# Attention in pairs of head pairs on quadrants of the PE array, and a last product with 512 tokens moving

## The chip, the cores and the metric

The kernel runs on one core of a Trainium2 chip. Times are device microseconds (us) of one execution. The runs shown are three, with median 1648.64 us (1648.32 to 1651.41); a profile of one further execution gives the instructions of each engine: PE (matmul), PEld (weight load), DVE (vector), ACT (scalar), POOL, and SP, whose queue issues the DMAs. PE, DVE, ACT and SP each work through a list of their own in order; semaphores tie the lists together.

## What is computed

The shapes are: 8 batches, 8 heads, 576 tokens, head size 64; then 4608 tokens of width 512, a first MLP of width 2048 and a gated second one of width 1536.

```python
def _attn_ref(q, k, v):
    q_s = softmax(q, axis=-1); k_s = softmax(k, axis=2)
    kv = np.einsum('bhsd,bhse->bhde', k_s, v)
    return np.einsum('bhsd,bhde->bhse', q_s, kv)
x = attn_out.transpose(0, 2, 1, 3).reshape(4608, 512)
x = np.maximum(x @ moe_w_in, 0.0) ** 2 @ moe_w_out
out = (1 / (1 + np.exp(-(x @ moe2_w_gate))) * (x @ moe2_w_val)) @ moe2_w_out
```

The `softmax` here stands for the maximum, the exponential, the sum with 1e-9 and the division that the reference writes out. The weights arrive as 64-bit floats.

## The kernel before, in words

**The order of the work.** Every piece of work is given to a planner (`Plan`) with a due time, its cost on an engine, what it must follow and which buffers it takes and gives. `plan.trace()` plays a clock through this list and emits the instructions in the order that comes out, so each engine's list, SP's included, is fixed when the program is built. The `plan_*` functions hold these due times and costs. `SIZES` says how many buffers each tag has; `W` is the pool of 512 KB weight buffers, eleven of them, and `X` and `S` are the pools of split activations.

**Numbers.** A float32 matrix is split into a high and a low part (ACT writes the high one, DVE the low one). A product is then three matmuls (`mm3`, L218 to L220) into one PSUM bank. Big products run as seven block products in place of eight (`PRODUCTS`, `plan_seven`); `s1`, `s5`, `s2` and `p4` are the four blocks of a result, of which `p4` ends last.

**Attention** (L408 to L676) goes in blocks: `j` counts nine blocks of 512 tokens, `b` eight batches, `p` four pairs of heads. For one (b, p), `plan_k` takes the column maximum of k (`k_max`, a PE transpose `k_turn`, `k_col`, a PE broadcast `k_all`), subtracts, exponentiates, and `k_mm` (L472) multiplies k by v: for each head the stationary matrix has 128 rows and 64 columns, so the two heads of the pair stand on the two column halves of the array. `k_copy` writes the two 64x64 results, scaled, on the diagonal of a 128x128 tile `kvf` whose other half is zero. For one (j, p), `plan_q` does the softmax of q on DVE and ACT; for j of 2 and more a head is spread over two groups of partitions, and `q_swap` (L534) brings the other group's maximum or sum by a small matmul. `q_mm` (L595) multiplies `kvf` by q: one full-array float32 matmul per piece of batch.

**The MLPs.** Blocks 0 to 2 go through the first MLP by `conv_in` and `conv_out`, while the weights are still being converted. The other six go in three stages (`in_stage`), with the attention of later blocks set between their matmuls. Five stages of the second MLP follow (`gate_stage`); four have 1024 tokens and the last 512. The end of a gate stage is `p_out2` (L736): y is stationary (128 tokens), a row block of `w_out2` moves, 256 columns at a time. Its results lie with tokens on partitions; `z_copy` and `z_st` (L942, L945) store them.

Of the kernel before, what the change touches and what calls it, by code (L numbers as in the profile page):

```python
# [142 lines left out]
def attention_mlp_mlp(  # L143
# [20 lines left out]
    nc = tc.nc  # L164
# [13 lines left out]
    SIZES = {"X": 14, "W": 11, "S": 6, "f": 19, "x": 8, "q": 3, "a": 6, "w": 5, "k": 2, "v": 2, "km": 1, "kr": 2, "pa": 2, "cb": 2, "qm": 4, "qr": 4}  # L178
# [12 lines left out]
    kvf = [[cst.tile([128, 128], F32, name=f"kv{a}{p}") for p in range(NP)] for a in range(2)]  # L191
# [233 lines left out]

# [6 lines left out]

    def k_max(b, p, r):

        kt = kt_t[b, p].rearrange("p r c -> p (r c)")
        C = 2 * D
        if r == 0:
            mx = cst.tile([128, 2 * C], F32, tag="kmx", name="kmx")
            nc.vector.tensor_tensor(out=mx, in0=kt[:, 0:2 * C], in1=kt[:, 2 * C:4 * C], op=ALU.max)
            kmx[b, p] = mx  # L440
            return
        a, c = kmx[b, p][:, 0:C], kmx[b, p][:, C:2 * C]
        nc.vector.tensor_tensor(out=a, in0=a, in1=kt[:, 4 * C:5 * C] if r == 1 else c, op=ALU.max)
        if r == 2:
            kmx[b, p] = a

    def k_turn(b, p):
        ps = banks[p] if b == 0 else pa.tile([128, N], F32, tag="pa", name="kps")
        nc.tensor.transpose(ps[:, KT0:KT0 + 128], kmx[b, p], ident)  # L449
        kps[b, p] = ps  # L450

    def k_col(b, p):

        m1 = sp.tile([128, 1], F32, tag="km1", name="km1")
        nc.vector.tensor_reduce(out=m1, in_=kps[b, p][:, KT0:KT0 + 128], axis=AX.X, op=ALU.max)
        kmx[b, p] = m1

# [14 lines left out]
    def k_mm(b, p):  # L472
        kt, vt = kt_t.pop((b, p)), vt_t.pop((b, p))
        ps = kps[b, p]
        for r in range(RK):
            for h in range(2):
                c = VC * r + (D + 2 if h else 1)
                nc.tensor.matmul(  # L478
                    ps[D * h:D * h + D, D - D * h:2 * D + 1 - D * h], kt[:, r, D * h:D * h + D], vt[:, c:c + D + 1],
                    start=(r == 0), stop=(r == RK - 1), skip_group_check=True,  # L480
                )

    def k_rec(b, p):
        ri = sp.tile([128, 1], F32, tag="kri", name="kri")
        nc.vector.tensor_scalar(out=ri, in0=kps[b, p][:, D:D + 1], scalar1=1e-9, scalar2=None, op0=ALU.add)
# [3 lines left out]
    def k_copy(b, p):  # L489
        ps, ri = kps.pop((b, p)), kmx.pop((b, p))  # L490
        for h in range(2):
            s = slice(D * h, D * h + D)
            c = slice(0, D) if h else slice(D + 1, 2 * D + 1)
            nc.scalar.activation(out=kvf[b % 2][p][s, s], in_=ps[s, c], func=AF.Copy, scale=ri[s])
# [47 lines left out]
    def q_both(j, p, op):  # L542
        st = q_st[j, p]
        n = N // qu_cols(j)
        s2 = st.rearrange("p g o -> p (g o)")
        if j >= NPE:
            nc.vector.tensor_tensor(out=s2, in0=s2, in1=q_ps.pop((j, p))[:, 0:n], op=op)
        return st, s2

    def q_sub(j, p):  # L550
        n = qu_cols(j)
        t = q_t[j, p].rearrange("p (g d) -> p g d", d=n)
        mx, _ = q_both(j, p, ALU.max)
        nc.vector.tensor_tensor(out=t, in0=t, in1=mx.to_broadcast([128, N // n, n]), op=ALU.subtract)
# [18 lines left out]
    def q_mul(j, p):  # L573
        n = qu_cols(j)
        t = q_t[j, p].rearrange("p (g d) -> p g d", d=n)
        nc.vector.tensor_tensor(out=t, in0=t, in1=q_rec.pop((j, p)).to_broadcast([128, N // n, n]), op=ALU.mult)

    def q_turn(j, p):
        t = tile2("a", "qtr")
        nc.vector.transpose(out=t, in_=q_t.pop((j, p)))  # L580
        q_ps[j, p] = t

    def q_turn_pe(j, p):
        t = q_t.pop((j, p)).rearrange("p (r c) -> p r c", r=R)
# [35 lines left out]
    SLACK = 2.14  # L620
    slack = lambda j: SLACK if j > 4 else 0.0

    def plan_k(b, p, key, step, wait=()):
        n = (b, p)
        big = ("W", "W") if b == 0 else ("k", "v")
        bank = [] if b == 0 else ["pa"]
        add(key - 5 if b else p, {DMA: 0.92}, ("kt",) + n, k_load, b, p, after=wait, take=big[:1])
        add(key - 4 if b else p + 4, {DMA: 0.92}, ("vt",) + n, v_load, b, p, after=wait, take=big[1:])
        add(key + 2.5 * step, {ACT: 0.22}, ("vo",) + n, v_ones, b, p, after=[("vt",) + n])
        add(key, {DVE: 0.34}, ("km0",) + n, k_max, b, p, 0, after=[("kt",) + n], take=["km"])  # L630
        add(key + 0.1, {DVE: 0.21}, ("km1",) + n, k_max, b, p, 1, after=[("km0",) + n])
        add(key + 0.2, {DVE: 0.21}, ("kmx",) + n, k_max, b, p, 2, after=[("km1",) + n])
        add(key + 0.5 * step, {PE: 0.14}, ("kt2",) + n, k_turn, b, p, after=[("kmx",) + n], take=bank, slack=slack(b))
        add(key + step, {DVE: 0.22}, ("kdg",) + n, k_col, b, p, after=[("kt2",) + n])
        add(key + 1.5 * step, {PE: 0.25}, ("kgm",) + n, k_all, b, p, after=[("kdg",) + n], give=["km"], slack=slack(b))
        add(key + 2 * step, {DVE: 0.74}, ("ks",) + n, k_sub, b, p, after=[("kgm",) + n])
        add(key + 3 * step, {ACT: 0.64}, ("ke",) + n, k_exp, b, p, after=[("ks",) + n])
        add(key + 4 * step, {PE: 0.65}, ("kp",) + n, k_mm, b, p, after=[("ke",) + n, ("vo",) + n], give=big, slack=slack(b))
        add(key + 5 * step, {DVE: 0.35}, ("kr",) + n, k_rec, b, p, after=[("kp",) + n], take=["kr"])
        add(  # L640
            key + 6 * step, {ACT: 0.65}, ("kv",) + n, k_copy, b, p,
# [763 lines left out]
```

## Time and profile before

| what | value |
|---|---|
| median of 3 runs | 1648.64 us |
| the profiled execution, its own time | 1648.78 us |
| its span, first instruction to last | 1647.0 us |
| PE busy | 1619.0 us, 98% |
| DVE busy | 1225.3 us, 74% |
| ACT busy | 942.4 us, 57% |
| DMA | 462.14 MB, mean 281 GB/s |
| HBM read and written | 364.54 MB, 95.94 MB |

The 1.8 us between the profiled time and its span lie before the first and behind the last instruction. A matmul's end in the profile is modelled and overlaps the next one, so the rate of PE is read from one start to the next and not from the durations. A float32 matmul stands in the profile as two matmuls (two passes), an `mm3` as three.

### The profile page before, as it was taken

To read this page: it belongs to the slowest core of one execution; us is meant where nothing else is said; L and a number is where in the kernel's file an instruction comes from. 1 tells how busy PE (TensorE), PEld (TensorE's weight loads), DVE (VectorE), ACT (ScalarE), POOL (GpSimd) and SP (SyncE) were. 2 spreads that over 40 slices of the span, in tenths; PEclk is the share of its full clock that TensorE was granted. 3 is DMA by queue.
4 is the path that set the end of the run, shared out by engine and by line. 5 is a ranking of instruction groups with operands and counts; after the bars stand their busy time and mean duration, and the time that the engine had idled before them with its cause. 6 is when DMAs were issued, how large, how long until landed. Compare 5 with 4: busy or idle time off the path is not lost.

```text
span 1647.0 us, 24974 instructions
## 1 busy us (share of the span) xinstructions
PE 1619.0 (98%) x8964; PEld 1377.5 (84%) x8964; DVE 1225.3 (74%) x2279; ACT 942.4 (57%) x1706; POOL 1.9 (0%) x14
## 2 busy tenths in 40 slices
PE   6899999999999999999999999999999999999999
PEld 4678888888888887888788899888988899889998
DVE  7988675999999999987996785447724783458446
ACT  5887665569585867675864464335523553335344
POOL 0000000000000000000000000000000000000000
PEclk8999999999999999999999999999999999999999
DMA  7695999999899979899989877656765667555896
GB/s 268 243 351 198 357 327 354 325 339 382 311 349 328 324 254 327 301 363 351 344 310 348 311 262 232 211 195 208 232 230 192 203 197 239 193 193 180 265 372 255
DMA packets 154331, 462.14 MB, mean 281 GB/s; under 512 B 16224, under 2 KB 25440, under 8 KB 154208
## 3 DMA queue, kind: packets, MB, share of 16 engines
q1 hardware_dynamic: 154208, 460.55, 79.7%
q8 instruction: 71, 1.16, 0.3%
q14 instruction: 52, 0.43, 0.1%
HBM read 364.54 MB, written 95.94 MB: 280 GB/s over the span
## 4 chain that ended last, share of the span: by engine, by line
PE 95%; DVE 2%; ACT 2%; DMA 1%; issue 0%; SPq 0%; ACTq 0%; DVEq 0%
PE bank L218 30%; PE bank L219 30%; PE bank L220 30%; PE xps L599 2%; PE kps L478 1%; PE qsw L539 1%; DMA vt<-in_v_dram 0%; PE kps L461 0%; DMA qt<-in_q_dram 0%; ACT wf L255 0%; PE qps L587 0%; PE bank L478 0%; PE kps L449 0%; DVE wf L285 0%; ACT whl L212 0%
## 5 line engine op out<-in xcount | busy, mean ns | idle before, releaser
L218 PE MATMUL bank<-bX,ws 128*128 128x512 f32 (+1 forms) x1176 | 444.6, 378 | 0.0
L219 PE MATMUL bank<-bX,ws 128*128 128x512 f32 (+1 forms) x1176 | 440.2, 374 | 0.0
L220 PE MATMUL bank<-bX,ws 128*128 128x512 f32 (+1 forms) x1176 | 440.0, 374 | 0.0
L756 DVE TENSOR_TENSOR s<-s,bank 128x512 f32<-128x512 f32 (+1 forms) x297 | 191.1, 651 | 190.7 <-PE bank L220 155.0
L212 ACT ACTIVATE s<-bank 128x512 f32<-128x512 f32 (+1 forms) x297 | 168.2, 571 | 205.4 <-PE bank L220 198.9
L212 ACT ACTIVATE bS<-s 128x512 fp32r<-128x512 f32 (+1 forms) x330 | 194.3, 600 | 134.1 <-PE bank L220 124.2
L215 DVE TENSOR_TENSOR bS<-s,bS 128x512 fp32r<-128x512 f32 (+1 forms) x330 | 212.7, 652 | 60.6 <-ACT bS L212 60.2
L220 PEld LDWEIGHTS bank<-bX,ws 128*128 128x128 f32 x1176 | 221.5, 188 | 40.0
L218 PEld LDWEIGHTS bank<-bX,ws 128*128 128x128 f32 x1176 | 221.9, 189 | 38.3 <-issue 0.2
L219 PEld LDWEIGHTS bank<-bX,ws 128*128 128x128 f32 x1176 | 221.7, 189 | 37.5 <-issue 0.2
L218 PE MATMUL bank<-ws,bS 128*128 128x256 f32 x756 | 214.0, 283 | 0.0
L219 PE MATMUL bank<-ws,bS 128*128 128x256 f32 x756 | 213.9, 283 | 0.0
L220 PE MATMUL bank<-ws,bS 128*128 128x256 f32 x756 | 213.9, 283 | 0.0
L775 ACT ACTIVATE s<-s 128x512 f32<-128x512 f32 (+1 forms) x120 | 70.5, 588 | 143.7 <-DVE s L756 143.5
L218 PEld LDWEIGHTS bank<-ws,bS 128*128 128x128 f32 x756 | 145.0, 192 | 1.2 <-ACT s L212 0.3
L219 PEld LDWEIGHTS bank<-ws,bS 128*128 128x128 f32 x756 | 145.0, 192 | 0.7
L220 PEld LDWEIGHTS bank<-ws,bS 128*128 128x128 f32 x756 | 145.1, 192 | 0.0
L218 PE MATMUL bank<-bS,ws 128*128 128x512 f32 x336 | 134.6, 401 | 0.7 <-ACT bS L212 0.3
L219 PE MATMUL bank<-bS,ws 128*128 128x512 f32 x336 | 131.2, 391 | 0.9 <-DVE bS L215 0.9
L220 PE MATMUL bank<-bS,ws 128*128 128x512 f32 x336 | 131.1, 390 | 0.0
L694 DVE TENSOR_TENSOR s<-s,s 128x512 f32<-128x512 f32 (+1 forms) x192 | 121.7, 651 | 1.9 <-ACT s L762 0.5
L212 ACT ACTIVATE whl<-wf 128x512 fp32r<-128x512 f32 x127 | 78.1, 625 | 40.2 <-DVE wf L299 12.1
(117 smaller groups left out, 2375.7 us busy)
## 6 DMA issues: line engine op xcount, KB each, us to landing
ws<-w_out SPq DMA_DIRECT2D x221, 512.0 KB, 5.1
ws<-w_gv SPq DMA_DIRECT2D x210, 512.0 KB, 4.4
ws<-w_in SPq DMA_DIRECT2D x100, 512.0 KB, 6.2
w_out<-whl SPq DMA_DIRECT2D x53, 512.0 KB, 4.6
w_gv<-whl SPq DMA_DIRECT2D x42, 512.0 KB, 5.2
w_in<-whl SPq DMA_DIRECT2D x32, 512.0 KB, 4.5
wraw<-in_moe_w_out_dram SPq DMA_DIRECT2D x28, 512.0 KB, 6.7
vt<-in_v_dram SPq DMA_DIRECT2D x32, 325.0 KB, 5.8
```

The lines of the kernel that those rows point to most:

```text
L212: nc.scalar.activation(out=dst, in_=src, func=AF.Copy)
L215: by_name[engine].tensor_tensor(out=dst, in0=src, in1=hi.bitcast(F32), op=ALU.subtract)
L218: nc.tensor.matmul(ps, ah, bh, start=first, stop=False, skip_group_check=True)
L219: nc.tensor.matmul(ps, ah, bl, start=False, stop=False, skip_group_check=True)
L220: nc.tensor.matmul(ps, al, bh, start=False, stop=last, skip_group_check=True)
L478: nc.tensor.matmul(ps[D * h:D * h + D, D - D * h:2 * D + 1 - D * h], kt[:, r, D * h:D * h + D], vt[:, c:c + D + 1], start=(r == 0), stop=( ...
L539: nc.tensor.matmul(ps[:, 0:n], swap, st.rearrange("p g o -> p (g o)"), start=True, stop=True)
L599: nc.tensor.matmul(ps[:, e], kvf[b % 2][p], t[:, e], start=True, stop=True)
L694: by_name[engine].tensor_tensor(out=t[o], in0=t[a], in1=t[b], op=ALU.subtract)
L756: nc.vector.tensor_tensor(out=t, in0=t, in1=banks[pr[b]][:, 0:n], op=ALU.add)
L775: nc.scalar.activation(out=t, in_=t, func=AF.Sigmoid)
```

## The change

1. Attention works on two pairs of heads at once. All DVE and ACT steps of k and q take twice the columns; the small PE steps are issued in twos. The odd pair of a double pair is loaded with its two heads exchanged. `kvf` is now 128x64, without zeros, and `q_mm` issues four 64x64 matmuls per piece of batch, one on each quadrant, into two PSUM banks by row half. Since the heads come out in another order, the rows of `w_in` are exchanged when it is loaded: three DMAs for one.
2. `p_out2` has the block of `w_out2` stationary and 512 tokens of y moving (256 in the last stage). Its result has features on partitions, so DVE turns it in 32x32 blocks (`z_turn`), `w_out2` is loaded in an order that fits (four DMAs for one, in pieces of 256 bytes), and each of the four result blocks is stored by four DMAs in pieces of 256 bytes.
3. Buffers, due times and costs of the planner are other ones.

```diff
-    SIZES = {"X": 14, "W": 11, "S": 6, "f": 19, "x": 8, "q": 3, "a": 6, "w": 5, "k": 2, "v": 2, "km": 1, "kr": 2, "pa": 2, "cb": 2, "qm": 4, "qr": 4}
+    SIZES = {"X": 14, "W": 11, "S": 6, "f": 19, "x": 8, "q": 2, "a": 6, "w": 5, "k": 2, "km": 1, "kr": 2, "pa": 2, "cb": 2, "qm": 2, "qr": 2}
-    kvf = [[cst.tile([128, 128], F32, name=f"kv{a}{p}") for p in range(NP)] for a in range(2)]
+    kvf = [[cst.tile([128, D], F32, name=f"kv{a}{p}") for p in range(NP)] for a in range(2)]
+        if kind == "in":
+            for a in range(2):
+                for c in range(1 + a):
+                    dst, at = (slice(256 * c, 256 * c + 256), slice(256 - 256 * c, 512 - 256 * c)) if a else (slice(0, 512),) * 2
+                    nc.sync.dma_start(out=t[64 * a:64 * a + 64, dst], in_=src[64 * a:64 * a + 64, at])
+            return
+        if kind == "out2":
+            for c in range(0, 512, 128):
+                part = src[:, c // 256].rearrange("p (a m k) -> p m a k", m=2, k=32)[:, c // 128 % 2]
+                nc.sync.dma_start(out=t[:, c:c + 128].rearrange("p (a k) -> p a k", k=32), in_=part)
+            return
     def k_mm(b, p):
+        for n in range(2):
+            vt = vt_t.pop((b, 2 * p + n))
+            for r in range(RK):
+                for g in range(2):
+                    h = g ^ n
+                    c = VC * r + (D + 2 if h else 1)
+                    o = KC * n + D - D * h
+                    nc.tensor.matmul(
+                        ps[D * g:D * g + D, o:o + D + 1], kt[:, n, C * r + D * h:C * r + D * h + D], vt[:, c:c + D + 1],
     def q_load(j, p):
+        nc.sync.dma_start(out=t[:, 0], in_=q[j, 2 * p])
+        src = q[j, 2 * p + 1]
+        for a in range(2):
...
+            nc.sync.dma_start(out=to, in_=at)
     def q_mm(j, p):
+        t = [q_ps.pop(("x", j, 2 * p + n)) for n in range(2)]
+        ps = [pa.tile([128, N], F32, tag="pa", name="xps") for _ in range(2)]
         for e, b in segs(j):
-            nc.tensor.matmul(ps[:, e], kvf[b % 2][p], t[:, e], start=True, stop=True)
+            for a, n in ((0, 0), (1, 0), (0, 1), (1, 1)):
+                row, col = slice(D * a, D * a + D), D * (a ^ n)
+                nc.tensor.matmul(ps[a][col:col + D, e], kvf[b % 2][2 * p + n][row], t[n][row, e], start=True, stop=True, skip_group_check=True)
-    def p_out2(use, yn, i, kk, pr, nk, nm):
+    def p_out2(use, yn, i, kk, pr, nk, n):
         w = whl[use]
-        c = slice(256 * (kk % 2), 256 * (kk % 2) + 256)
         y = bs[yn + (kk,), i]
-        for m in range(nm):
-            ps = banks[pr[m // 2]][:, 256 * (m % 2):256 * (m % 2) + 256]
-            t = slice(128 * m, 128 * m + 128)
-            mm3(ps, y[:, 0, t], y[:, 1, t], w[:, 0, c], w[:, 1, c], i in OPENS and kk == 0 and m % 2 == 0, kk == nk - 1)
+        for m in range(2):
+            ps = banks[pr[m]][:, 0:n] if n == N else banks[pr[0]][:, n * m:n * m + n]
+            c = 256 * (kk % 2) + 128 * m
+            mm3(ps, w[:, 0, c:c + 128], w[:, 1, c:c + 128], y[:, 0], y[:, 1], i in OPENS and kk == 0 and (m == 0 or n == N), kk == nk - 1)
+    def z_turn(uid, nm, b, n, src):
...
+        for m in (b,) if n == N else range(2):
+            nc.vector.transpose(out=zt[uid, nm][:, :, m, :], in_=t if n == N else t[:, n * m:n * m + n])
-    def z_st(uid, nm, b, row, col, n):
-        dst = out[row + 256 * b:row + 256 * b + 256, col:col + 256].rearrange("(m p) c -> p m c", p=128)
-        nc.sync.dma_start(out=dst, in_=t.rearrange("p (m c) -> p m c", m=2))
+    def z_st(uid, nm, row, col, n):
+        for a in range(4):
+            dst = out[row:row + n, col + 64 * a:col + 64 * a + 64].rearrange("(b i) c -> i b c", i=32)
+            nc.sync.dma_start(out=dst, in_=t[32 * a:32 * a + 32].rearrange("i b m k -> i b (m k)"))
...
-                plan_w(kind, g, T4 + 24.29 + (t + 126.34 - T4 - 24.29) / len(preps) * m, 10.0, "w")
+                plan_w(kind, g, T4 + 39.9 + (t + 126.34 - T4 - 39.9) / len(preps) * m, 10.0, "w")
```

**Where instructions move, at three places.** First PE at the program's start, up to the first `mm3` of `conv_in`. The names are those of the tiles: `kmx` and `km` are the maxima, `vt` and `kt` values and keys, `qps` the turned q, `xps` the product with `kv`. Before:

```order
L449 MATMUL bank_88<-ident,kmx 128x128
L461 MATMUL bank_88<-ident,km_134 128x128
L587 MATMUL qps<-ident,qt 128x128 x4
L478 MATMUL bank_88<-vt,kt 64x65 x10
L449 MATMUL bank_89<-ident,kmx 128x128
L461 MATMUL bank_89<-ident,km_190 128x128
L599 MATMUL xps<-qf_178,kv_80 128x512
```

Now:

```order
L469 MATMUL bank_88<-ident,kmx 128x128 x2
L482 MATMUL bank_88<-ident,km_127 128x128 x2
L503 MATMUL bank_88<-vt,kt 64x65 x20
L617 MATMUL qps<-ident,qt 128x128 x4
L469 MATMUL bank_89<-ident,kmx 128x128 x2
L617 MATMUL qps<-ident,qt 128x128 x4
L482 MATMUL bank_89<-ident,km_218 128x128 x2
L631 MATMUL xps<-qf_208,kv_80 64x512 x2
L631 MATMUL xps<-qf_223,kv_81 64x512 x2
```

The four single chains, one for each pair, have become two double ones; a 128x512 matmul of `q_mm` for each pair has become four of 64x512 for two pairs.

Second, PE at the first `p_out2` of the first gate stage, one step of one product (`bS` is y, `ws` the fetched weights). Before, with buffer numbers:

```order
L218 MATMUL bank4_92<-ws_9394,bS_8927 128x256
L219 MATMUL bank4_92<-ws_9394,bS_8927 128x256
L220 MATMUL bank4_92<-ws_9394,bS_8927 128x256
...
L218 MATMUL bank5_93<-ws_9394,bS_8927 128x256
L219 MATMUL bank5_93<-ws_9394,bS_8927 128x256
L220 MATMUL bank5_93<-ws_9394,bS_8927 128x256
...
```

Now:

```order
L218 MATMUL bank4_92<-bS_8577,ws_9079 128x512
L219 MATMUL bank4_92<-bS_8577,ws_9079 128x512
L220 MATMUL bank4_92<-bS_8577,ws_9079 128x512
L218 MATMUL bank5_93<-bS_8577,ws_9079 128x512
L219 MATMUL bank5_93<-bS_8577,ws_9079 128x512
L220 MATMUL bank5_93<-bS_8577,ws_9079 128x512
```

Before, each of the two triples stands twice in a row: such a step was twelve matmuls of 256 columns, and is six of 512.

Third, DVE where the first gate stage ends and the second begins (`s` are the result blocks in SBUF, `p` is `p4`, `bX` the split input of the next stage). Before:

```order
L756 TENSOR_TENSOR s_9975<-s_9975,bank_88 128x512
L756 TENSOR_TENSOR s_9977<-s_9977,bank_89 128x512
L751 COPY p_10353<-bank_93 128x512
L756 TENSOR_TENSOR s_10203<-s_10203,bank_92 128x512
L756 TENSOR_TENSOR s_10273<-s_10273,bank_93 128x512
```

Now:

```order
L215 TENSOR_TENSOR bX<-x2r,bX 128x512 x6
L741 TENSOR_TENSOR x2r<-x2r 128x512 x2
L999 STREAM_TRANSPOSE zt<-s_9447 128x16x32
L999 STREAM_TRANSPOSE zt<-s_9449 128x16x32
L215 TENSOR_TENSOR bX<-x2r,bX 128x512 x2
L999 STREAM_TRANSPOSE zt<-bank_92 128x16x32
L999 STREAM_TRANSPOSE zt<-bank_93 128x16x32
L215 TENSOR_TENSOR bX<-x2r,bX 128x512
L802 TENSOR_TENSOR s_9704<-s_9704,bank_90 128x512
```

The transposes of the results stand among the splits of the next stage's input, and the two that read `p4` from PSUM stand ahead of the last split and of the next stage's first sum.

## Rows read from the trace of the kernel before

**Rows 1.** The page: PE in the whole, its costliest group of `p_out2`, the chain's shares.

```profile
PE 1619.0 (98%) x8964; PEld 1377.5 (84%) x8964; DVE 1225.3 (74%) x2279; ACT 942.4 (57%) x1706; POOL 1.9 (0%) x14
...
PE 95%; DVE 2%; ACT 2%; DMA 1%; issue 0%; SPq 0%; ACTq 0%; DVEq 0%
...
L218 PE MATMUL bank<-ws,bS 128*128 128x256 f32 x756 | 214.0, 283 | 0.0
```

**Rows 2.** Busy time by stretch: length, PE, PEld, DVE, ACT, POOL, PEclk, DMA share, GB/s.

```profile
0.00:33.30 33.30, 17.84 (x116) 10.79 (x117) 26.71 (x67) 20.57 (x42) 1.87 (x14) 0.87 0.70 249
33.30:110.00 76.70, 69.78 (x388) 52.03 (x387) 67.89 (x156) 55.81 (x105) 0.00 (x0) 0.92 0.82 294
450.00:537.00 87.00, 86.64 (x436) 70.09 (x435) 85.11 (x161) 63.44 (x115) 0.00 (x0) 1.00 0.94 336
705.00:967.00 262.00, 260.80 (x1149) 215.00 (x1148) 213.11 (x359) 166.16 (x288) 0.00 (x0) 1.00 0.93 334
1555.00:1612.00 57.00, 57.00 (x477) 57.00 (x477) 27.42 (x71) 23.63 (x60) 0.00 (x0) 1.00 1.00 373
```

**Rows 3.** Timeline of PE in `p_out2`: start, duration, line, tiles.

```profile
1009.79 0.28 PE L218 MATMUL bank<-ws,bS 128*128 128x256 f32 x1
...
1015.79 0.28 PE L220 MATMUL bank<-ws,bS 128*128 128x256 f32 x1
```

**Rows 4.** Timeline of PE in an `in_stage`, with one `q_swap` (L539).

```profile
560.45 0.39 PE L220 MATMUL bank<-bX,ws 128*128 128x512 f32 x1
...
563.17 0.39 PE L220 MATMUL bank<-bX,ws 128*128 128x512 f32 x1
563.40 0.29 PE L539 MATMUL qsw<-qst,swap 128*128 128x16 f32 x2
...
564.09 0.39 PE L220 MATMUL bank<-bX,ws 128*128 128x512 f32 x1
```

**Rows 5.** The same, around one `k_mm` (L478).

```profile
578.48 0.39 PE L220 MATMUL bank<-bS,ws 128*128 128x512 f32 x1
578.80 0.80 PE L478 MATMUL kps<-vt,kt 128*64 128x65 f32 x20
579.53 0.50 PE L218 MATMUL bank<-bS,ws 128*128 128x512 f32 x1
...
580.10 0.40 PE L220 MATMUL bank<-bS,ws 128*128 128x512 f32 x1
```

**Rows 6.** The same, around one `q_mm` (L599).

```profile
415.06 0.39 PE L220 MATMUL bank<-bS,ws 128*128 128x512 f32 x1
415.29 1.02 PE L599 MATMUL xps<-qtr,kv 128*128 128x320 f32 x4
...
416.61 0.40 PE L220 MATMUL bank<-bS,ws 128*128 128x512 f32 x1
```

**Rows 7.** The same, around one `k_all` (L461).

```profile
591.73 0.39 PE L220 MATMUL bank<-bS,ws 128*128 128x512 f32 x1
591.96 0.38 PE L461 MATMUL kps<-ident,km 128*128 128x128 f32 x2
...
592.64 0.40 PE L220 MATMUL bank<-bS,ws 128*128 128x512 f32 x1
```

**Rows 8.** Groups by line and shape: engine time, then mean ns of one.

```profile
L215 DVE TENSOR_TENSOR bS<-s,bS 128x512 fp32r<-128x512 f32 x288 | 195.3, 685 | 55.4 <-ACT bS L212 55.2
...
L215 DVE TENSOR_TENSOR bS<-s,bS 128x256 fp32r<-128x256 f32 x42 | 17.5, 422 | 5.2 <-ACT bS L212 5.0
```

**Rows 9.** Timeline of PE at the first `mm3`, and of SP's last store.

```profile
33.32 1.42 PE L218 MATMUL bank<-x,whl 128*128 128x512 f32 x1
...
1643.93 0.37 SPq L948 DMA_DIRECT2D out_dram<-p  x1
```

**Rows 10.** Stretches as in rows 2: the last store alone; weight fetches alone.

```profile
1643.90:1646.10 2.20, 0.00 (x0) 0.00 (x0) 0.00 (x0) 0.00 (x1) 0.00 (x0) 0.93 0.35 119
...
1560.00:1600.00 40.00, 40.00 (x336) 40.00 (x335) 19.82 (x52) 17.14 (x44) 0.00 (x0) 1.00 1.00 377
```

More of the change, by code (lines that the diff above doesn't have):

```diff
@@ L441, in k_max @@
             return
[L442 to L445, printed above, removed]
+        mx = kmx[b, p]
+        nc.vector.tensor_tensor(out=mx, in0=mx, in1=kt[:, :, C * r + C:C * r + 2 * C], op=ALU.max)
     def k_turn(b, p):
-        ps = banks[p] if b == 0 else pa.tile([128, N], F32, tag="pa", name="kps")
-        nc.tensor.transpose(ps[:, KT0:KT0 + 128], kmx[b, p], ident)
@@ L490, in k_copy @@
         ps, ri = kps.pop((b, p)), kmx.pop((b, p))
[L491 to L494, printed above, removed]
+        for n in range(2):
+            for g in range(2):
+                s = slice(D * g, D * g + D)
+                c = KC * n + (0 if g ^ n else D + 1)
+                nc.scalar.activation(out=kvf[b % 2][2 * p + n][s], in_=ps[s, c:c + D], func=AF.Copy, scale=ri[s, n:n + 1])
     def segs(j):
@@ L624, in plan_k @@
         n = (b, p)
-        big = ("W", "W") if b == 0 else ("k", "v")
+        vs = [(b, 2 * p + x) for x in range(2)]
         bank = [] if b == 0 else ["pa"]
[L627 to L639, printed above, removed]
-        add(
-            key + 6 * step, {ACT: 0.65}, ("kv",) + n, k_copy, b, p,
+        if b:
+            add(key - 5, {DMA: 3.7}, ("kt",) + n, kv_load, b, p, after=wait, take=["k", "k"])
+        else:
+            add(p, {DMA: 1.84}, ("kt",) + n, k_load, b, p, take=["k"])
@@ new lines, in plan_k @@
+        for x in vs:
+            if not b:
+                add(p + 4, {DMA: 0.92}, ("vt",) + x, v_load, *x, take=["W"])
+            add(key + 2.5 * step, {ACT: 0.22}, ("vo",) + x, v_ones, *x, after=[("kt",) + n if b else ("vt",) + x])
+        for r in range(RK - 1):
+            add(
+                key + 0.1 * r, {DVE: 0.35}, ("km",) + n + (r,), k_max, b, p, r,
+                after=[("km",) + n + (r - 1,) if r else ("kt",) + n], take=[] if r else ["km"],
+            )
+        add(key + 0.5 * step, {PE: 0.25}, ("kt2",) + n, k_turn, b, p, after=[("km",) + n + (RK - 2,)], take=bank, slack=slack(b))
@@ new lines, in plan_k @@
+        add(key + step, {DVE: 0.35}, ("kdg",) + n, k_col, b, p, after=[("kt2",) + n])
+        add(key + 1.5 * step, {PE: 0.46}, ("kgm",) + n, k_all, b, p, after=[("kdg",) + n], give=["km"], slack=slack(b))
+        add(key + 2 * step, {DVE: 1.4}, ("ks",) + n, k_sub, b, p, after=[("kgm",) + n], give=bank)
+        add(key + 3 * step, {ACT: 1.15}, ("ke",) + n, k_exp, b, p, after=[("ks",) + n])
+        add(
+            key + 4 * step, {PE: 1.22}, ("kp",) + n, k_mm, b, p, after=[("ke",) + n] + [("vo",) + x for x in vs],
+            take=bank, give=["k"] + (["k"] if b else ["W", "W"]), slack=slack(b),
+        )
@@ L642, in plan_k @@
+        add(key + 5 * step, {DVE: 0.36}, ("kr",) + n, k_rec, b, p, after=[("kp",) + n], take=["kr"])
+        add(
+            key + 6 * step, {ACT: 1.3}, ("kv",) + n, k_copy, b, p,
             after=[("kr",) + n] + (kv_users[b - 2, p] or [("kv", b - 2, p)] if b > 1 else []), give=["kr"] + bank,
@@ L1000, in conv_in @@
                 add(t, {FREE: 0.0}, ("cx", j, kt), lambda: None, after=[("ch", j, z, kt) for z in range(F1)], give=[XTAG[j]])
-        add(t + 5.56, {ACT: 1.17}, ("cg", j, f), c_g, j, f, after=[("ch", j, f, KT - 1)], take=[gtag(j, f)], give=["cb"])
+        add(t + 8.33, {ACT: 1.17}, ("cg", j, f), c_g, j, f, after=[("ch", j, f, KT - 1)], take=[gtag(j, f)], give=["cb"])
     def conv_out(j, f, t):
@@ L1010, in conv_out @@
             conv_fetch(j, "out", g, ii, t)
-        add(t - -0.96, {ACT: AS}, ("chi", j, f), c_hi, j, f, after=[("cg", j, f)], take=["S"])
+        add(t - -0.04, {ACT: AS}, ("chi", j, f), c_hi, j, f, after=[("cg", j, f)], take=["S"])
         add(t - 2, LOW, ("clo", j, f), c_lo, j, f, CHOSEN, after=[("chi", j, f)], give=[gtag(j, f)])
@@ L1040, in plan_blocks @@
             done_b.update(new)
-            for p in range(NP):
+            for p in range(NP // 2):
                 for b in new:
@@ L1044, in plan_blocks @@
                 plan_q(j, p, t + 2.0, 0.99)
-                t += per / NP
+                t += 2 * per / NP
+    turns = []
     def plan_x(nm, js, t, src, n):
-        xorder.extend(("bhi", nm + (kk,), i) for i in PRODUCTS for kk in range(2))
+        own = [("bhi", nm + (kk,), i) for i in PRODUCTS for kk in range(2)]
+        xorder.extend(turns[:1] + own[:4] + turns[1:2] + own[4:10] + turns[2:3] + own[10:12] + turns[3:] + own[12:])
+        turns.clear()
         for kk in range(2):
@@ L1120, in load @@
             k_ = key(nm, b)
-            add(t - 11.19, {DMA: 0.8}, ("old",) + k_, o_ld7, k_, (uid, nm, b), after=[("ost",) + k_ + (0,), ("p", ("u1", n, 1, 1), 3, 1)], take=["a"])
+            add(t - 5.62, {DMA: 0.8}, ("old",) + k_, o_ld7, k_, (uid, nm, b), after=[("ost",) + k_ + (0,), ("p", ("u1", n, 1, 1), 3, 1)], take=["a"])
             return ("old",) + k_
@@ L1292, in pe @@
                 )
-                t += 3 * nm_ * MH
-            return [nm] * (nm_ // 2), t
-        end, prs, t = plan_seven(uid, t, nm_ // 2, N, pe, {x: ["a", "a"] for x in ("s1", "s5", "s2")})
+                t += 6 * mm
+            return [nm] * nb, t
+        end, prs, t = plan_seven(uid, t, nb, N, pe, {x: ["a", "a"] for x in ("s1", "s5", "s2")})
         fin = []
         rows = [N * j for j in js] if len(js) > 1 else [N * js[0], N * js[0] + nt]
-        for b in range(nm_ // 2):
-            nm = ("e", uid, "p4", b)
-            add(t, {ACT: AP, DVE: TT}, nm, z_copy, uid, prs[0], b, N, "a", CHOSEN, after=[end["p4"][b]], take=["a"])
-            fin.append(nm)
-            for key, c, ch in (("s1", 0, 0), ("s2", 1, 0), ("p4", 0, 1), ("s5", 1, 1)):
-                last = nm if key == "p4" else end[key][b]
-                add(t + 1, {DMA: 0.8}, ("zst", uid, key, b), z_st, uid, key, b, rows[c], 256 * ch, N, after=[last], give=["a"])
+        for key, c, ch in (("s1", 0, 0), ("s5", 1, 1), ("s2", 1, 0), ("p4", 0, 1)):
+            turned = []
+            for b in range(nb):
+                src = banks[prs[0][b]] if key == "p4" else None
+                nm = ("zt", uid, key, b)
+                add(
+                    t + 0.5, {DVE: 0.65 if nb > 1 else 0.8}, nm, z_turn, uid, key, b, nt, src, after=[end[key][b]] + turned,
+                    take=[] if b else ["X"], give=[] if key == "p4" else ["a"],
+                )
+                turned = [nm]
+                if not b:
+                    turns.append(nm)
+                if key == "p4":
+                    fin.append(nm)
+            add(t + 1, {DMA: 1.0}, ("zst", uid, key), z_st, uid, key, rows[c], 256 * ch, nt, after=turned, give=["X"])
         freed[prs[0]] = (t, fin)
```

231 lines of the change are left out of this document (122 added, 109 removed).

## The prediction

> **What bounds the kernel now.** I read the page first, then the spans by stretch, then single instructions of PE. The page shows PE busy for 1619.0 us, 98% of the span, DVE at 74%, ACT at 57%, and a chain of waits that is 95% PE [rows 1]. By stretch: from 110 us on PE is full wherever one looks, with little spare elsewhere: DVE is busy for 85.1 of 87 us in 450 to 537, the DMA share is 0.93 in 705 to 967, and 1.00 in the last gate stages, where 57.0 of 57 us are PE's [rows 2]. Only the first 33.3 us belong to loads and to DVE (26.7 us busy against 17.8 on PE), and up to 110 us PE still lacks 6.9 of 76.7 us [rows 2]. So the time is PE's list of work laid end to end. I price what the change takes from that list, from one start to the next, and then look for what could make PE wait. The profiled execution took 1648.78 us, 0.14 above the median of the runs; its span is 1647.0.
>
> **The last product.** In 1009.79 to 1015.79 lie 50 intervals between `p_out2` matmuls of 256 columns: 6.00/50 = 0.120 us each [rows 3]. A 512-column matmul of an `in_stage` costs (563.17 - 560.45)/12 = 0.227 us [rows 4]. Three such groups, one for each line of `mm3`, have 756 matmuls each [rows 1]: 2268. A ninth, 252, belongs to the last stage and keeps 256 columns; the other 2016 become 1008. Each saves 2 x 0.120 - 0.227 = 0.013 us: 1008 x 0.013 = **-13.1 us**. The Trainium skill ("TensorE: Matmul & The Clock Gate", "Wait — 56ns, not 53.3ns?") puts the fixed part of a warm matmul at about 2.5 ns; by that alone the saving would be an estimated 2.5 us (rival C). The rows show 13 ns, about five times it, and the rows decide.
>
> **Attention between the matmuls.** An insertion costs the time between its neighbours less three times 0.227 us, i.e. 0.68, where three matmuls follow it.
> - `q_swap`: 564.09 - 563.17 - 0.68 = 0.24 [rows 4]. 56 become 28: **-6.6**.
> - `k_mm`: 1.62 - 0.68 = 0.94; its 20 records of 65 columns take 0.73 of it [rows 5]. A double one issues 40 behind the same lead-in: 0.94 + 0.56 = 1.50, with 0.56 from the next item. 14 doubles in place of 28: 14 x (1.88 - 1.50) = **-5.3**.
> - `q_mm`: 1.55 - 0.68 = 0.88 for 512 columns in two passes, 0.87 ns per column and pass [rows 6]. At that rate the 20 x 65 columns of `k_mm` would take 1.13 us one after the other; they take 0.73 with lead-in [rows 5], so the two column halves of the array work at once: 0.565 for the work, 0.37 around it. The new `q_mm` does two pairs on four quadrants. If all four run at once it streams 512 columns twice, 0.88, with 0.37 around it: 1.25, in place of 2 x 0.88. Sixteen such doubles stand between matmuls: 16 x 0.51 = **-8.2**. That row halves, too, run at once no row shows. The bounds are 1.25 and, serial, four times 0.88 plus 0.37 = 3.9. I take the lower end because the column halves, the nearest row, do overlap.
> - `k_all` costs 0.91 - 0.68 = 0.23 [rows 7]; with `k_turn`, a matmul half as long, about 0.36 per pair, and a double about 0.64, since only lead-ins are shared: 14 x (0.72 - 0.64) = **-1.2**.
>
> **The start.** Four single chains become two double ones. A 512-column split takes DVE 685 ns and a 256-column one 422 ns [rows 8], so 2 x 422 - 685 = 159 ns of each DVE instruction is fixed. Some eleven merged instructions per double pair save 1.8 us, two doubles 3.6. Against that the first k load is twice as big (320 KB at the 249 to 294 GB/s of these stretches [rows 2], about +1), and the first chain, twice as wide, ends later (+1). The first `mm3` now starts at 33.32 us, and the granted clock around it is 0.87 and then 0.92 of full, partly at 1.2 in place of 2.4 GHz [rows 2, 9]. I add the waits that PE's list sheds up to 110 us and take **-2.5**, between -6 and +3.
>
> **The end.** SP's last store is now issued at 1643.93, and the span ends at 1647.0 [rows 9]. In place of one ACT copy of `p4` and one issue there are two DVE transposes from PSUM and four issues. I price a transpose by the nearest row, a DVE pass over 256 columns, 0.42 [rows 8], and an issue by SP's 0.37 [rows 9]: 2 x 0.42 - 0.4 + 3 x 0.45, about **+1.8** (0 to +3).
>
> **Hidden work.** `z_turn` in the four big stages is 16 passes of at most 1 us on a DVE that is busy for 27 of 57 us there [rows 2]; without this cover it would delay the splits that the next stage waits for. The extra loads of `w_in` and q are some 50 issues of SP at 0.4 us; each can only hold up the weight fetch behind it, which is issued well before its use.
>
> **The 256-byte pieces.** `w_out2`'s twelve loads become 2048 packets each for 256, and each gate stage's results 8192 for 2048. No row shows a packet of 256 bytes. The last store was 256 packets of 1 KB: 0.35 x 16 engines x 2.2 us / 256 = 48 ns each; a weight fetch moves 4 KB in about 174 ns (16 engines, 377 GB/s) [rows 10]. A line through both gives 16.5 ns for 256 bytes and 90 for 2 KB; the upper end is 48 ns, as if size saved nothing. In 705 to 967 the engines have 0.07 x 262 = 18 us free [rows 2]. Over 16 engines the twelve loads bring 12 x (2048 x 16.5 - 256 x 90)/16 ns = 8 us: it fits. At 48 ns they bring 56 us, 38 more than is free. The Trainium skill ("DMA: Bandwidth & Descriptors", "Specifications") wants at least 512 bytes for line rate and has a read-modify-write below; this rule speaks against the change. In the last gate stages, share 1.00, stores delay fetches straight away, with eleven buffers as cushion. I take **+3** (0 to 15 with the line's price, more in the rival).
>
> The sum: -13.1 - 6.6 - 5.3 - 8.2 - 1.2 - 2.5 + 1.8 + 3 = -32.1; from 1648.6 that is **1616.5 us**.
>
> **The rivals.**
> (A) Row halves take turns in `q_mm`. For: two loads of weights for the same columns, and no row shows it. Against: the halves have their own rows and PSUM banks. Price 16 x 0.9 = +14: 1631. Fully serial, 16 x 2.65 = +42: 1659, slower. The Trainium skill ("TensorE: Matmul & The Clock Gate", "Part 3: Packing small matmuls — row/col tiling") has matmuls on different row groups overlap.
> (B) The small packets starve PE: the place is 705 to 967 and the last gate stages, the mechanism that a load of `w_out2` holds the DMA engines and the fetches behind it come late. A packet of p ns adds 1.54 x p - 17 us there, so the 18 us of slack are gone at 23 ns; at 48 ns the stall is 38 us: 1651 with the +3 of the sum left out, **slower than before**. It decides at about 46 ns, where the stall eats the other 35 us of gain. For: share 0.93 to 1.00 [rows 2]. Against: time per packet falls with size in every pair of rows that I have [rows 10].
> (C) The fixed part of a matmul is not what sets 0.120 us (a load of weights may), and a longer moving side gives back only a fifth: -2.5 in place of -13.1: 1627.
> (D) DVE becomes the bound at 450 to 537, where 1.9 us are free [rows 2]. The merging frees DVE as well, 1.8 us for each double pair, so I expect no more than +5: 1622.
>
> **How the numbers follow.** Forecast, with small slips in the start, the end and the stores: 66%, own range 1606 to 1626. A at +14: 10%; serial: 2%. B: 6% slower than before, 7% for a mild form at 1621 to 1640. C: 7%. D: 2%. From 1605 to 1636 leaves out the slower cases and a start and end better than I priced, together under 20%. About 0.2%, 3.3 us, is what a measurement can tell from no change. Slower by more than that: serial and most of B, 0.07; within: 0.03; faster: 0.90.
>
> **What would show it.** In the trace after: `p_out2` starts 0.227 us apart; half as many groups of `q_swap`, each costing 0.24; a `k_mm` of 40 records near 1.5 us; a `q_mm` near 1.25 with pairs or fours of starts a few ns apart (2.1 or more is A); the first `mm3` near 31 us. Gaps on PE before L218 that a fetched weight ends, in 705 to 967 or after 1500 us, with the DMA share at 1.00, are B. DVE as the releaser of PE in 450 to 537 is D. If the time lies under 1605, the insertions cost more than I read, or the start shed more waits; over 1636, a queue that I called hidden was not.

## The result and the profile after

The changed kernel takes 1626.05 us (median of 4 runs, 1624.17 to 1632.12) beside 1648.97 for the kernel before on the same chip: a ratio of 0.9865 with a 95% interval of 0.9836 to 0.9894 (ratios go by all runs, not by the medians), and 22.9 us faster by the medians. The forecast was 1616.5, 32.1 us faster. The profiled execution took 1624.61 us with a span of 1622.8. Its page, in the lines that answer to [rows 1]:

```profile
PE 1586.1 (98%) x8028; PEld 1306.0 (80%) x8028; DVE 1226.5 (76%) x2099; ACT 929.5 (57%) x1663; POOL 0.7 (0%) x6
...
PE 83%; DVE 6%; DMA 6%; ACT 2%; SPq 2%; issue 1%; DVEq 0%; ACTq 0%
PE bank L218 27%; PE bank L219 27%; PE bank L220 27%; DMA out_dram<-zt 2%; DVE bS L215 1%; DMA wraw<-in_moe_w_in_dram 1%; PE xps L631 1%; DMA qt<-in_q_dram 1%; PE kps L503 1%; DVE bX L215 1%; DMA xp<-xp 1%; DMA w_in<-whl 1%; SPq L1005 0%; DVE xp L802 0%; DMA vt<-in_v_dram 0%
...
L218 PE MATMUL bank<-bX,ws 128*128 128x512 f32 (+1 forms) x1176 | 444.0, 378 | 5.5 <-ACT bX L212 4.2
```

PE still shows 98%, but the chain that was 95% PE is 83% now, and the largest new piece is a store: `out_dram<-zt`, 2%. The matmuls of L218 with input `bX` (the first products of the gate stages and of the `in_stage`s) had no idle time before them and now have 5.5 us, 4.2 of them ended by an ACT split of `bX`.

The stretches that answer to [rows 2], in the same columns (length, PE, PEld, DVE, ACT, POOL, PEclk, DMA share, GB/s), moved to where the same work now stands:

```profile
0.00:32.89 32.89, 16.80 (x124) 10.82 (x125) 23.66 (x42) 17.80 (x33) 0.70 (x6) 0.82 0.98 258
32.89:110.00 77.11, 69.23 (x431) 52.93 (x429) 70.27 (x129) 60.12 (x111) 0.00 (x0) 0.94 0.95 311
433.00:520.00 87.00, 86.84 (x441) 69.94 (x441) 83.13 (x143) 61.65 (x112) 0.00 (x0) 1.00 0.96 343
683.00:944.00 261.00, 260.70 (x1149) 215.30 (x1149) 206.51 (x346) 159.99 (x277) 0.00 (x0) 1.00 0.97 335
1531.00:1588.00 57.00, 56.35 (x468) 55.95 (x467) 28.67 (x75) 23.58 (x62) 0.00 (x0) 1.00 1.00 371
```

In 683 to 944 the DMA share rose from 0.93 to 0.97, and PE is as full as before: the loads of `w_out2` in 256-byte pieces fit. Of the stretches behind 110 us only the last shows PE short by more than 0.3 us.

**Where the 24.2 us between the two spans come from.** A table of starts, from the timelines of PE (us; "gate 1" is the first matmul behind the last product of the stage before the first gate stage, and so on; 24 to 30 of a gate stage's own matmuls run before that point, between those of the last product; the two columns on the right belong to experiments told below):

| | before | changed | attention alone | zt in own buffers |
|---|---|---|---|---|
| first `mm3` | 33.32 | 32.89 | 29.87 | 32.38 |
| gate 1 | 858.16 | 835.67 | 835.35 | 837.78 |
| gate 2 | 1034.33 | 1008.94 | 1011.52 | 1010.50 |
| gate 3 | 1209.17 | 1182.17 | 1186.36 | 1181.86 |
| gate 4 | 1384.01 | 1355.33 | 1361.20 | 1353.22 |
| gate 5 | 1555.55 | 1527.89 | 1532.74 | 1521.47 |
| last matmul | 1642.99 | 1617.44 | 1620.20 | 1608.92 |
| end of span | 1647.0 | 1622.8 | 1624.3 | 1614.3 |

Up to gate 1 the change gains 22.5 us. From there to the last matmul it gains only 784.83 - 781.77 = 3.1 us, though the four `p_out2` got shorter as forecast: 204 of them in a row start from 945.02 to 991.03, 46.01/203 = 0.227 us apart.

```profile
945.02 0.39 PE L218 MATMUL bank<-bS,ws 128*128 128x512 f32 x1
...
991.03 0.39 PE L220 MATMUL bank<-bS,ws 128*128 128x512 f32 x1
```

The rest was given back at the start of each following stage. The waits of PE from 1000 to 1620 us (engine and line, what it waited for: us in total, times, longest) name it:

```profile
PE bank L218 <- ACT bX L212: 4.2, 4, 1.8
PE bank L218 <- ACT s L212: 0.7, 1, 0.7
PE bank L219 <- DVE bX L215: 0.7, 3, 0.2
```

And the timeline at the start of gate 2, first ACT, then one line of DVE, then SP and PE (start, duration, engine, line, tiles; in brackets the idle time before and what ended it):

```profile
1010.50 0.60 ACT L212 ACTIVATE s<-bank 128x512 f32<-128x512 f32 x1 [2.12 <-PE bank L220]
1014.18 0.63 ACT L212 ACTIVATE bX<-x2r 128x512 fp32r<-128x512 f32 x1 [3.08 <-DMA out_dram<-zt]
1016.77 0.63 ACT L821 ACTIVATE s<-s 128x512 f32<-128x512 f32 x1 [1.96 <-DVE s L802]
1019.55 0.63 ACT L212 ACTIVATE bX<-x2r 128x512 fp32r<-128x512 f32 x1 [2.15 <-DMA out_dram<-zt]
...
1008.46 1.40 DVE L999 STREAM_TRANSPOSE zt<-bank 128x512 f32<-128x512 f32 x2 [1.98 <-PE bank L220]
...
1009.89 2.70 SPq L985 DMA_DIRECT2D x2r<-x  x2
1012.69 0.38 SPq L319 DMA_DIRECT2D ws<-w_gv  x1
1013.17 2.25 SPq L1005 DMA_DIRECT2D out_dram<-zt  x4
...
1018.91 0.39 PE L220 MATMUL bank<-bX,ws 128*128 128x512 f32 x1
1020.24 0.50 PE L218 MATMUL bank<-bX,ws 128*128 128x512 f32 x1 [0.94 <-ACT bX L212]
1020.96 0.50 PE L219 MATMUL bank<-bX,ws 128*128 128x512 f32 x1 [0.22 <-DVE bX L215]
```

The chain of waits says the same (start, duration, what), with the last of the four issues and its landing:

```profile
1014.12 0.59 SPq L1005
1014.76 4.73 DMA out_dram<-zt
1019.55 0.64 ACT bX L212
```

A split of the next stage's input waits for a **store of the stage before**. `z_turn` writes its result `zt` into a buffer of the `X` pool, the pool of the splits `bX`. The buffer is free only when the four stores have landed: `z_turn` of `p4` is over at 1009.86, SP starts the four issues from 1013.17 to 1014.76, behind two input loads and a fetch; the last lands at 1019.48, and the split follows at 1019.55. PE wanted it at 1019.14. Beyond 0.227 us per matmul, PE lost 1.9 us there, 1.8 at gate 3, 4.3 at gate 4 and 2.1 in gate 5: 10.1 together. (The expectations below were written with 1.8, 1.8, 4.2 and 2.1, 9.9 together.) At gate 4 the waits themselves are 2.7 us; behind them PE's granted clock fell to 0.50 (the lower of two levels, 1.2 GHz), which cost some 1.5 more. The first wait there, two starts at the low clock, and a stretch of it (columns as in [rows 2]):

```profile
1365.30 0.39 PE L220 MATMUL bank<-bX,ws 128*128 128x512 f32 x1
1367.46 0.50 PE L218 MATMUL bank<-bX,ws 128*128 128x512 f32 x1 [1.77 <-ACT bX L212]
...
1370.05 0.63 PE L219 MATMUL bank<-bX,ws 128*128 128x512 f32 x1
1370.47 0.63 PE L220 MATMUL bank<-bX,ws 128*128 128x512 f32 x1
...
1369.90:1372.60 2.70, 2.70 (x7) 2.06 (x7) 2.51 (x5) 0.69 (x2) 0.00 (x0) 0.50 0.95 360
```

### The profile page after: what moved, and what is told of

The parts are those of the page before. It is cut to its first block, busy times and chain, and to the rows that moved or that the text cites. A ratio compares the mean times of both kernels' runs of the same rounds, so it can differ in the third digit from the quotient of the medians.

```text
span 1622.8 us, 23027 instructions
## 1 busy us (share of the span) xinstructions
PE 1586.1 (98%) x8028; PEld 1306.0 (80%) x8028; DVE 1226.5 (76%) x2099; ACT 929.5 (57%) x1663; POOL 0.7 (0%) x6
## 4 chain that ended last, share of the span: by engine, by line
PE 83%; DVE 6%; DMA 6%; ACT 2%; SPq 2%; issue 1%; DVEq 0%; ACTq 0%
PE bank L218 27%; PE bank L219 27%; PE bank L220 27%; DMA out_dram<-zt 2%; DVE bS L215 1%; DMA wraw<-in_moe_w_in_dram 1%; PE xps L631 1%; DMA qt<-in_q_dram 1%; PE kps L503 1%; DVE bX L215 1%; DMA xp<-xp 1%; DMA w_in<-whl 1%; SPq L1005 0%; DVE xp L802 0%; DMA vt<-in_v_dram 0%
## 5 line engine op out<-in xcount | busy, mean ns | idle before, releaser
L218 PE MATMUL bank<-bX,ws 128*128 128x512 f32 (+1 forms) x1176 | 444.0, 378 | 5.5 <-ACT bX L212 4.2
L218 PE MATMUL bank<-bS,ws 128*128 128x512 f32 (+1 forms) x756 | 287.6, 380 | 0.0
L219 PE MATMUL bank<-bS,ws 128*128 128x512 f32 (+1 forms) x756 | 285.9, 378 | 0.4 <-DVE bS L215 0.4
L220 PE MATMUL bank<-bS,ws 128*128 128x512 f32 (+1 forms) x756 | 285.5, 378 | 0.0
L218 PEld LDWEIGHTS bank<-bX,ws 128*128 128x128 f32 x1176 | 221.8, 189 | 49.3 <-ACT bX L212 5.6
L218 PEld LDWEIGHTS bank<-bS,ws 128*128 128x128 f32 x756 | 142.3, 188 | 28.1 <-issue 1.7
L219 PEld LDWEIGHTS bank<-bS,ws 128*128 128x128 f32 x756 | 142.4, 188 | 26.7 <-DVE bS L215 1.7
L220 PEld LDWEIGHTS bank<-bS,ws 128*128 128x128 f32 x756 | 142.3, 188 | 26.5
L215 DVE TENSOR_TENSOR whl<-wf,whl 128x512 fp32r<-128x512 f32 x127 | 86.3, 689 | 18.0 <-ACT whl L212 16.0
L215 DVE TENSOR_TENSOR bX<-x2r,bX 128x512 fp32r<-128x512 f32 (+1 forms) x70 | 41.8, 631 | 29.2 <-ACT bX L212 29.2
L266 ACT ACTIVATE wf<-wraw 128x512 f32<-128x512 f32 x68 | 45.0, 664 | 24.2 <-DMA wraw<-in_moe_w_out_dram 16.9
```

Of the source, the lines that this page charges most:

```text
L215: by_name[engine].tensor_tensor(out=dst, in0=src, in1=hi.bitcast(F32), op=ALU.subtract)
L218: nc.tensor.matmul(ps, ah, bh, start=first, stop=False, skip_group_check=True)
L219: nc.tensor.matmul(ps, ah, bl, start=False, stop=False, skip_group_check=True)
L220: nc.tensor.matmul(ps, al, bh, start=False, stop=last, skip_group_check=True)
L266: nc.scalar.activation(out=t, in_=high.bitcast(F32), func=AF.Abs)
```

## The experiments

Theory T says: what is lost are X buffers, held until the stores land. Rival D: the new transposes stand in DVE's way. Rival P: packets of 256 bytes make the DMA engines late. (This D is not the prediction's, which stood for DVE as the bound in 450 to 537.)

**zt in buffers of its own.**

```diff
+    ZTAG = {"s1": "q", "s5": "q", "s2": "k", "p4": "k"}
-            zt[uid, nm] = tile4("X", "zt", F32, (128, n // 32, 2, 32))
+            zt[uid, nm] = tile2(ZTAG[nm], "zt", (128, n // 32, 2, 32))
```

The planner's takes and gives of `X` for these steps follow. As these splits need not wait now, the planner sets the last two of a stage's opening ones ahead of the copy that stood before them: beside the buffers, the order of ACT's list changes at this place. (With the 1 KB stores below, that order stays as in the changed kernel.)

> The four result blocks turned by z_turn (zt) get buffers of their own, namely the q and k buffers that attention has left, in place of X buffers. Nothing else is changed. Theory T (the lost 10 us are the X buffers: the splits of the next stage's input wait until the stores of zt have landed): the gaps of PE at the starts of gate stages 2 to 5, 1.8 + 1.8 + 4.2 + 2.1 us in the changed kernel, go below 0.5 us each, and the profiled execution falls from 1624.6 to about 1615.5 (1613 to 1618). Rival D (the new transposes stand in DVE's list ahead of the splits): the gaps stay at 8 us or more, released by DVE, 1623 to 1625. Rival P (256-byte packets make the DMA engines late, so that the input loads x2r land late): the gaps stay at 5 us or more, released by a DMA of x2r, 1620 to 1625.

Measured: 1616.64 us (1616.10 to 1618.90, 5 runs), ratio 0.9803 (0.9790 to 0.9817). From 1000 us on the view of waits has no row for PE. At gate 2, ACT now splits without waiting for a store (the same view as above):

```profile
1009.83 1.14 ACT L212 ACTIVATE bX<-x2r 128x512 fp32r<-128x512 f32 x2
1012.05 0.60 ACT L212 ACTIVATE s<-bank 128x512 f32<-128x512 f32 x1 [1.08 <-PE bank L220]
```

The transposes and the small packets are all still there, so neither D nor P alone is the cause of what is lost at the gates. Stages 1 to 4 are 3.3 to 3.5 us shorter than before, each (table: 176.17 - 172.72, 174.84 - 171.36, and so on), 13.7 us together. The median is 9.4 us under the changed kernel's, and the interval lies wholly below those of the changed kernel and of attention alone. (The profiled executions differ by 8.5 us: 10.6 less lost in the gate stages, but gate 1 comes 2.1 later, and no run here says why.)

**The part on attention alone.** `p_out2`, the stores and the loads of `w_out2` are those of before:

```diff
-    def p_out2(use, yn, i, kk, pr, nk, n):
+    def p_out2(use, yn, i, kk, pr, nk, nm):
...
-    def z_st(uid, nm, row, col, n):
+    def z_st(uid, nm, b, row, col, n):
```

> Only the part on attention: p_out2, the stores and the loads of w_out2 are those of before. If the two parts add up, the time falls by what the changed kernel has gained by the first gate matmul, 22.5 us: 1648.8 - 22.5 = 1626.3 (1624 to 1628), and the gate stages last 784.8 us as before. If attention's gain rests on the other part (less DMA or DVE work in common), it falls by less than 20 us.

Measured: 1625.37 us (4 runs), ratio 0.9851 (0.9837 to 0.9864). The gain of 22.8 us stands at gate 1, and the gate stages last 784.85 us as before (table). Attention alone is thus as fast as the whole change.

**The part on the last product alone.** `p_out2`, `z_turn`, `z_st`, the loads of `w_out2` and the planner's numbers for the gate stages are those of the change; attention is that of before.

```diff
-            mm3(ps, y[:, 0, t], y[:, 1, t], w[:, 0, c], w[:, 1, c], i in OPENS and kk == 0 and m % 2 == 0, kk == nk - 1)
+            mm3(ps, w[:, 0, c:c + 128], w[:, 1, c:c + 128], y[:, 0], y[:, 1], i in OPENS and kk == 0 and (m == 0 or n == N), kk == nk - 1)
```

> Only the part on the last product: p_out2 with 512 tokens moving, z_turn, the stores and the loads of w_out2; attention is that of before. Theory T: four times -3.45 us in p_out2, +9.9 us of gaps at the starts of stages 2 to 5, +1.4 us at the end: 1648.8 - 2.5 = 1646.3 (1643 to 1649). Rival P, if small packets also slow the conversion of the weights: slower than before, over 1650.

Measured: 1651.82 us (9 runs, 1646.94 to 1659.77), ratio 1.0020 (1.0004 to 1.0035). The sum was 5.5 us too good: the time lies outside the 1643 to 1649 of theory T and where rival P put it, over 1650. The profiled execution (1651.16) shows what was missing. Gates 2 to 5 lose 12.8 us against the kernel with own buffers, where the sum had 9.9; the first gate stage loses 0.9, and gate 1 comes at 859.25 us, 1.1 later than before; the sum had nothing for either. P has a small part in this: in 700 to 945 us PE loses 4.6 us, where the kernel before lost 2.0, and 1.9 of the 4.6 lie behind loads of `w_out2` in 256-byte pieces, which ACT had waited for (they landed at 792.07 and 923.27). The waits of PE behind 1000 us are the same kind and larger than in the changed kernel:

```profile
PE bank L218 <- ACT bX L212: 5.9, 3, 2.5
PE bank L218 <- ACT s L212: 1.6, 1, 1.6
PE bank L219 <- DVE bX L215: 0.7, 3, 0.2
```

These runs lie 12.8 us apart, those with own buffers 2.8. The longest has the lowest mean granted clock of the nine (0.988) and the shortest the highest (0.997), so stretches at the low clock, as behind gate 4 above, are likely a part of it. What the gaps cost in each run is open, since only one was profiled.

**Stores in pieces of 1 KB.** The content lands at other places of the output.

```diff
-            dst = out[row:row + n, col + 64 * a:col + 64 * a + 64].rearrange("(b i) c -> i b c", i=32)
-            nc.sync.dma_start(out=dst, in_=t[32 * a:32 * a + 32].rearrange("i b m k -> i b (m k)"))
+            dst = out[row + n // 4 * a:row + n // 4 * (a + 1), col:col + 256].rearrange("(i r) c -> i r c", i=32)
+            nc.sync.dma_start(out=dst, in_=t[32 * a:32 * a + 32].rearrange("i b m k -> i (b m k)").rearrange("i (r c) -> i r c", c=256))
```

> As the changed kernel, but each of the four stores of a result block writes pieces of 1 KB in place of 256 bytes: the same number of DMAs and bytes, from the same partitions, at other places of the output. Theory T: the buffers are still held; a store of four moves in 1.5 us in place of 2.4 us of all engines' time, so each of the four gaps shrinks by 1 us at most: 1620.5 to 1624. Rival P: the gaps go below 0.5 us each: 1614 to 1617.

Measured: 1619.79 us (4 runs, 1618.29 to 1620.79), ratio 0.9817 (0.9803 to 0.9830): between the two expectations, and better than T allowed. The last of the four stores before gate 2 took 3.4 us from issue to landing in place of 4.7. That was enough at gates 2 to 4: there gaps of 0.5 us at most are left; one wait remains, in gate 5, where 1.8 us are lost in all.

```profile
PE bank L218 <- ACT bX L212: 1.0, 1, 1.0
```

So the packets of the stores have a part in it, by way of the buffers that wait for them; and with ACT's order unchanged, an earlier landing alone nearly closes the gaps. Whether small store packets cost anything else, the next kernel shows.

**Own buffers and 1 KB pieces together**, the two edits above in one kernel.

> The kernel with own buffers for zt, and stores of 1 KB pieces in place of 256 bytes (at other places of the output). Theory T in the form after the first runs (small packets cost time only through the X buffers that wait for them): 1616.6 as with own buffers alone, within 1.5 us. If small packets cost PE time by another way as well: 1613 or less.

Measured: 1619.28 us (4 runs, 1616.00 to 1620.12), ratio 0.9808 (0.9790 to 0.9825). The median is 2.6 us above that of own buffers alone, more than the 1.5 expected, but the ratio's interval covers that of own buffers alone (0.9803), and nothing is gained. The two profiles agree: from gate 2 to the last matmul both kernels take 598.4 us. The one with both edits is 2.1 us later at gate 2 (1012.63), but it had lost these 2.1 before its first store of a result, at 1000.03; and behind the last matmul it took 6.1 us in place of 5.4. With the buffers out of the way, small **store** packets cost PE no time that these runs can show. The loads of `w_out2` have pieces of 256 bytes in every kernel with the new product, so what those cost is not shown by a run of its own; the profile of the last product alone gives 1.9 us.

**q_mm on one row half.** All four matmuls read the upper 64 rows of `kvf` and q, so the second half of the heads is left out.

```diff
-                nc.tensor.matmul(ps[a][col:col + D, e], kvf[b % 2][2 * p + n][row], t[n][row, e], start=True, stop=True, skip_group_check=True)
+                nc.tensor.matmul(ps[a][col:col + D, e], kvf[b % 2][2 * p + n][0:D], t[n][0:D, e], start=True, stop=True, skip_group_check=True)
```

> As the changed kernel, but all four matmuls of a piece in q_mm read the upper 64 rows (of kvf and of q), so that they stand on two quadrants of one row half in place of four; the second half of the heads is left out by this and the first taken twice. The order of all engines is the same. If row halves run at once (forecast), a q_mm now takes turns and costs about 0.37 + 2 x 0.88 = 2.1 us in place of 1.235: 16 x 0.9 = 14 us, about 1640 beside 1626.05. If the 1.235 us had another cause (a matmul of 64 rows is cheaper by itself), nothing changes: 1624 to 1628.

Measured: 1641.59 us (9 runs, 1635.07 to 1646.50), ratio 0.9954 (0.9941 to 0.9967), 15.5 us above the changed kernel. The same `q_mm` in the timeline of PE, in the changed kernel:

```profile
314.16 0.39 PE L220 MATMUL bank<-g0hl,ws 128*128 128x512 f32 x1
314.48 1.09 PE L631 MATMUL xps<-qtr,kv 64*64 64x256 f32 x16
...
316.07 0.39 PE L220 MATMUL bank<-g0hl,ws 128*128 128x512 f32 x1
```

and on one row half:

```profile
319.15 0.39 PE L220 MATMUL bank<-g0hl,ws 128*128 128x512 f32 x1
319.47 1.94 PE L631 MATMUL xps<-qtr,kv 64*64 64x256 f32 x16
...
321.93 0.40 PE L220 MATMUL bank<-g0hl,ws 128*128 128x512 f32 x1
```

By the rule of the sum these are 1.91 - 0.68 = 1.23 and 2.78 - 0.68 = 2.10 us. The same sixteen records on two quadrants take 0.87 us more, 13.9 for sixteen, so the gain rests on row halves that run at once.

## Why the prediction was right and where it failed

- **The last product**, -13.1: right. The four stages with own buffers are 13.7 us shorter than before. Rival C, with its 2.5 ns per matmul, is out: the interval is 0.227 against 0.120 us for half the columns.
- **q_mm**, 1.25: measured 1.23 in thirteen of the sixteen, 1.22 in two more. What rival A named as the sign of turns, 2.1, is what the one-row-half kernel shows, 2.10. One `q_mm`, at 67.3 us, cost 4.3, waits for ACT included.
- **k_mm**, 1.50: measured 1.53. **q_swap**, 0.24: 0.23. **k_all and k_turn**, 0.64 for a double: 0.45 and 0.23, together 0.68. (By the prediction's own numbers -6.6 should be -6.7 and -1.2 should be -1.1; the two slips cancel.)
- **The start**: the first `mm3` came at 32.89 and not near 31 (in the kernel with attention alone at 29.87). The sum of start and attention was -23.8; at gate 1 the profiles of the kernels with this attention show -22.5 (changed), -22.8 (attention alone), -20.4 (own buffers), -19.7 (1 KB stores) and -19.5 (both). Attention is the same in all five; why they differ by up to 3.3 us stays open.
- **The end**, +1.8: from 1617.44 to 1622.8 are 5.4 us, from 1642.99 to 1647.0 were 4.0: +1.3 by the unrounded times.
- **Rivals B and D** did not come as named: no wait of PE for a fetched weight in 683 to 944 or behind 1000 us, none for DVE in 433 to 520. A mild form of B did come, by another way: at 912.96 in the changed kernel PE lost 0.5 us to ACT, which had waited until a load of `w_out2` in 256-byte pieces landed at 911.83; with the last product alone 1.9 us were lost so, with own buffers alone none.
- **The step that failed** is the +3 of "The 256-byte pieces", and with it the sentence of "Hidden work" that `z_turn` is covered. The price of a packet was good: 16.5 ns estimated. In the changed kernel's last 3.2 us only the four last stores move, 1024 packets; the stretch below (columns as above) gives 0.38 x 16 x 3.2 us / 1024 = 19 ns. But I looked for the damage among the weight fetches, with eleven buffers as cushion, and counted DVE's time as the only cost of `z_turn`. I did not ask **which pool its result takes**. The result sits in `X` until it has been stored; the splits of the next stage, which need `X`, have no cushion of that size. Measured: 10.1 us at gates 2 to 5, and with the 0.5 of the first stage (behind the load named above) 10.6, in place of 3. In the profiled execution the sum closes: 1648.78 - 32.1 = 1616.7; 7.6 more for the gaps, 1.3 less gained at gate 1, 0.5 and 0.6 better at the end and in the last product make 1624.5, and it took 1624.61.

```profile
1618.60:1621.80 3.20, 0.00 (x0) 0.00 (x0) 0.00 (x0) 0.00 (x0) 0.00 (x0) 1.00 0.38 82
```

The Trainium skill ("DMA: Bandwidth & Descriptors", "Specifications") puts the size for line rate at 512 bytes. The stretch agrees in that its rate is 82 GB/s at a share of 0.38, some 216 GB/s for a full share, against some 340 for the 1 KB pieces of the last store before and 377 at 1.00 for fetches in pieces of 4 KB [rows 10]. For the stores it mattered here only through the buffers that waited.

**Luck.** 1626.05 lies between 1605 and 1636, but the prediction did not see the wait that put it there: no rival names it, and the room above the forecast was meant for other slips. That own buffers come to 1616.64, beside the forecast of 1616.5, is partly luck too: start and attention gave 20.4 of 23.8, and the +3 was not needed.

## What to carry to other kernels

A new step costs more than its engine's time: list each buffer that it takes, from which pool, until which event it is held, and who asks that pool next; where it is held until a store lands, the time of SP's queue and of the landing (here 3.3 and 6.3 us) is part of the step. A change of several parts is best split: here attention gave all of the gain, the last product gave back what it gained, and other buffers for one tile made it gain. For a list of PE that is full, the interval between starts around an insertion, read from one like it, prices a doubled insertion to a few hundredths of a microsecond.

## What the runs showed of the hardware

- Four 64x64 matmuls on four quadrants cost 1.23 us for 512 columns of two pairs, and 2.10 on two quadrants.
- Waits of 2.7 us in all on PE were followed by matmuls 0.43 us apart, at a granted clock of 0.50, for some 3 us; after waits of 1.8 us in the same kernel the clock stayed at full. With the last product alone, waits of 2.6 and 2.7 us left it at full, and 3.4 us were followed by a stretch at 0.54. The length of the waits alone thus does not tell which comes.
- A store packet of 256 bytes took 19 ns of one DMA engine, one of 1 KB 48 ns [rows 10].
